# Attention products on 64 by 64 quarters of the matmul array, two groups of rows a step

## The chip, the cores and the metric

The kernel runs on one core of a Trainium2 chip. The metric is the device time of one launch in microseconds (us), as the median of several runs. Five engines of the core work side by side, each with a queue of its own that it works off in order: TensorE (PE, and PEld for its weight loads), VectorE (DVE), ScalarE (ACT), GpSimd (POOL) and SyncE (SP), which issues most of the DMA transfers.

## The reference

Attention with heads mixed before and after the softmax, then two feed-forward layers.

```python
batch, n_heads, seq, head_dim = (2, 12, 448, 64)
scores = scale * np.matmul(q, k.transpose(0, 1, 3, 2))
scores = np.einsum('bhij,hg->bgij', scores, w_pre)
scores = scores - np.max(scores, axis=-1, keepdims=True)
attn = np.exp(scores)
attn = attn / (np.sum(attn, axis=-1, keepdims=True) + 1e-09)
attn = np.einsum('bhij,hg->bgij', attn, w_post)
return np.matmul(attn, v).astype(np.float32)
...
h = x @ w_in            # 896 x 768, 768 x 2048
g = h * relu6 / 6.0     # relu6 = clip(h + 3, 0, 6); the second layer: max(h, 0) + alpha * min(h, 0)
return (g @ w_out).astype(np.float32)
```

## The kernel before

The 448 query rows of each of the two batches are cut into four tiles of 120, 120, 120 and 88 rows, eight tiles `ti` in all. Attention works on **groups** of 10 query rows (`G`): 10 rows by 12 heads are 120 partitions (`GP`), and there are 90 groups (`NG`), 12 in a tile of 120 rows and 9 in one of 88.

- **Scores.** `qk` (L193) makes the scores of one head for one tile, 448 keys wide. The products are in float32r, in two matmuls that add into one bank: keys and queries are split beforehand into a rounded part and a rest (`split_k` L150, `split_k0` L156, `split_q` L165, on DVE and POOL), stacked on 128 partitions. The first tile, and half of the second, use `qk0` (L187): one plain float32 matmul over 64 partitions, the even heads on partitions 0 to 63 and the odd ones on 64 to 127. ACT copies each head out of the bank into the tile `S` (L599, L532).
- **Pull.** `pull` (L209) moves one group from `S` (query row on the partition) to 120 partitions of row and head, by a DMA from on-chip memory to on-chip memory that SP issues.
- **Mix.** `premix` (L225) multiplies a group by the 120 by 120 matrix `wpre`, which holds `w_pre` ten times on its diagonal, into a bank `mx` (two of them); DVE takes the negated maximum (L227); `exp` (L235) is one ACT instruction and a read of its running sum.
- **Post-mix.** `norm` (L216 to L219, DVE) scales the block-diagonal `wpost` by the reciprocal sums, and `post` (L245) multiplies: the weights are 112 keys of `e`, the moving operand the 120 columns of `wr`, four matmuls a group, into a bank `pt` (two); ACT copies it to `MT` (L258), now with keys on the partitions.
- **Values.** `av` (L282) multiplies `MT` by `v` for a pair of heads `a`: four blocks of 112 keys, the two heads in the two column halves of the array. Every three pairs are copied to `xT` (L295, DVE; for the last two tiles L290 and L291).

float32 matmuls are recorded as two instructions each ("passes" below). The main loop `for s_ in range(-PL, NG + LAG)` runs one step for each group, in code order on every engine: `premix(s_)`, the scores of about one head for the next tile, `exp(s_)`, the copies, `norm(s_ - 1)`, `post(s_ - 3)`. All six `av` of a tile stand in one step, five steps after the tile's last group. In the last steps of the loop, matmuls of the first feed-forward layer (`mm3`, L446) are put in; then come the two layers, float32r in three matmuls, which the diff leaves as they are.

Of the kernel before, what the change touches and what calls it, by code (L numbers as in the profile page):

```python
# [7 lines left out]
F32 = mybir.dt.float32  # L8
# [9 lines left out]
LAG = 3  # L18
PL = 4
# [16 lines left out]
def kernel(  # L36
# [15 lines left out]
    nc = tc.nc  # L52
# [24 lines left out]
    NTILE, NG = len(tiles), len(groups)  # L77
    tps = NTILE // B
# [22 lines left out]
    with tc.manual_schedule():  # L101
        xT = xtp.tile([128, KD, NT], F32, name="xT")
        k_st, v_t, q_st = {}, {}, {}

        def load_k(b, c):
            t = kq.tile([128, HC, S], F32, tag="kst", bufs=2, name="kst")
            nc.sync.dma_start(out=t, in_=k[b - 1, :, HC * c:HC * (c + 1), :])
            k_st[b, c] = t


        def load_k0(p, z, q=nc.sync):
            c = p // HC
            if (0, c) not in k_st:
                k_st[0, c] = kq.tile([128, HC, S], F32, tag="kst", bufs=2, name="kst")
            q.dma_start(out=k_st[0, c][:, p - HC * c:z - HC * c, :], in_=k0[:, p:z, :])

        load_k0(0, 1, nc.scalar)
# [4 lines left out]
        def load_q0(c):  # L122
            n = tiles[0]["n"]
            t = q_st[0, c] = kq.tile([128, HC * GP], F32, tag="qst", bufs=3, name="qst")
            for o in range(2):
                src = q[0, D * o:D * o + D, 2 * HC * c * n:2 * HC * (c + 1) * n]
                nc.sync.dma_start(  # L127
                    out=t[D * o:D * o + D, :HC * n].rearrange("p (j x) -> p j x", j=HC),
                    in_=src.rearrange("p (j o x) -> p j o x", j=HC, o=2)[:, :, o, :],
                )  # L130

        def load_v(b, c):
            t = late.tile([JP, HC, NJ, D], F32, tag=f"v{c}", bufs=1, name=f"v{c}")
            nc.sync.dma_start(out=t, in_=v[b, :, HC * c:HC * (c + 1)])
            v_t[b, c] = t

        def load_q(ti, c):
            T = tiles[ti]
            n = HC * T["n"]
            t = kq.tile([128, HC * GP], F32, tag="qst", bufs=3, name="qst")  # L140
            a = T["i0"] * H + c * n
            nc.sync.dma_start(out=t[:, :n], in_=q[T["b"], :, a:a + n])
            q_st[ti, c] = t

        kT = [None] * H
        qT, S_t, MT = {}, {}, {}

        def split_k(b, h):  # L150
            src = k_st[b, h // HC][:, h % HC, :]
            t = kT[h] = kq.tile([128, S], R, tag=f"kT{h}", name=f"kT{h}")
            nc.vector.tensor_copy(t, src)
            nc.gpsimd.tensor_tensor(t[D:], src[D:], t[D:].bitcast(F32), ALU.subtract)

        def split_k0(h):  # L156
            a, z = (0, D) if h % 2 == 0 else (D, 2 * D)
            src = k_st[0, h // 2 // HC][a:z, h // 2 % HC, :]
            t = kT[h] = kq.tile([128, S], R, tag=f"kT{h}", name=f"kT{h}")
            nc.gpsimd.tensor_scalar(t[a:z], src, 1.0, 1.0, ALU.mult, ALU.mult)  # L160
            nc.vector.tensor_tensor(
                t[D - a:2 * D - a], src, t[a:z].bitcast(F32), ALU.subtract
            )

        def split_q(ti, c, eng=nc.gpsimd):  # L165
            n = HC * tiles[ti]["n"]
            s = q_st.pop((ti, c))[:, :n]
            t = kq.tile([128, 2, HC * GP], R, tag="qT", bufs=3, name="qT")
            eng.tensor_scalar(t[:, 0, :n], s, 1.0, 1.0, ALU.mult, ALU.mult)
            eng.tensor_tensor(t[:, 1, :n], s, t[:, 0, :n].bitcast(F32), ALU.subtract)  # L170
            qT[ti, c] = t

        def qk_out(ti, h, other):
            n = tiles[ti]["n"]
            if h == 0:
                S_t[ti] = (s_odd if ti % 2 else s_even).tile([128, H, S], F32, tag="S", name="S")
            p = (psA if other else psB).tile(
                [GP, 512], F32, tag="mx" if other else "sc", bufs=2, name="sc"
            )
            return n, p  # L180


        def qk0(ti, h):
            n, p = qk_out(ti, h, h % 2)
            o, j = D * (h % 2), h // 2
            c, a = (h // HC, h % HC) if ti else (j // HC, j % HC)
            nc.tensor.matmul(  # L187
                p[:n, :S], q_st[ti, c][o:o + D, a * n:(a + 1) * n],
                k_st[0, j // HC][o:o + D, j % HC, :], start=True, stop=True,
            )  # L190
            return (S_t[ti][:n, h, :], p[:n, :S])

        def qk(ti, h, other=False):  # L193
            n, p = qk_out(ti, h, other)
            t = qT[ti, h // HC]
            a = (h % HC) * n
            for o in range(2):
                nc.tensor.matmul(  # L198
                    p[:n, :S], t[:, o, a:a + n], kT[h], start=(o == 0), stop=(o == 1)
                )  # L200
            return (S_t[ti][:n, h, :], p[:n, :S])
# [575 lines left out]
```

## Time and profile before

| | us |
|---|---|
| median of 3 runs (701.15 to 703.30) | 702.01 |
| profiled execution, its own time | 700.6 |
| its span, first to last instruction | 698.7 |
| PE busy in the span | 689.4 (99%) |
| ACT busy | 372.3 (53%) |
| DVE busy | 438.6 (63%) |
| POOL busy | 322.2 (46%) |

The profiled execution's 700.6 us and its span differ by 1.9 us that lie around the instructions. Busy shares are means over stages of different kind: the attention loop runs from the first `premix` at 17.9 us to the last `av` at 244.5 us, and what follows is the two layers.

### The profile page before, as it was taken

The page shows a single profiled execution, that of the slowest core. Times are in us where ns is not written, and L with a number is a line of the kernel's source. Part 1 is how long each engine was busy: PE and PEld are TensorE (multiplying, and loading weights), DVE is VectorE, ACT ScalarE, POOL GpSimd, SP SyncE. Part 2 cuts the span into 40 slices and gives each one's busy share as a digit, 9 for nine tenths or more (in the row PEclk, how much of TensorE's full clock was granted, in tenths as well). Part 3 has the DMA queues.
Part 4 walks back from the last instruction along what each step waited for, and adds up shares of the span by engine and source line. Part 5 has one row for each costly group of instructions (what it writes and reads, how often), then busy time and mean ns, then how long its engine had stood idle before and what let it go on. Part 6 is the DMA issues. An engine that isn't in the chain of part 4 may idle for free.

```text
span 698.7 us, 11159 instructions
## 1 busy us (share of the span) xinstructions
PE 689.4 (99%) x4164; PEld 608.6 (87%) x4164; DVE 438.6 (63%) x778; ACT 372.3 (53%) x692; POOL 322.2 (46%) x222
## 2 busy tenths in 40 slices
PE   7999999999999999999999999999999999999998
PEld 3678878878778999999999999999999999999997
DVE  5565884456765558888873454359999999435311
ACT  5785575676866656566544443344544444444300
POOL 6321652212225344555567554534555455775630
PEclk9999999999999999999999999999999999999999
DMA  5486543364536113323234423222223223445302
GB/s 153 172 222 193 187 122 115 128 176 158 189 63 162 46 46 118 110 94 132 91 135 136 137 91 135 91 91 90 91 95 130 94 91 104 154 149 186 119 1 79
DMA packets 31874, 85.20 MB, mean 122 GB/s; under 512 B 5966, under 2 KB 21966, under 8 KB 31822
## 3 DMA queue, kind: packets, MB, share of 16 engines
q1 hardware_dynamic: 31678, 84.28, 37.9%
q8 instruction: 33, 0.54, 0.3%
q10 hardware_dynamic: 144, 0.23, 0.1%
q14 instruction: 19, 0.16, 0.1%
HBM read 62.47 MB, written 2.75 MB: 93 GB/s over the span
## 4 chain that ended last, share of the span: by engine, by line
PE 88%; POOL 4%; issue 3%; DMA 1%; DVE 1%; ACT 1%; SPq 1%; POOLq 0%
PE p L446 59%; PE pt L245 10%; PE mx L225 9%; PE av L282 5%; PE sc L198 4%; POOL wb L369 2%; POOL wlo L380 2%; DMA kst<-in_k_dram 1%; SPq L209 0%; DVE nm L227 0%; ACT S L532 0%; DMA qst<-in_q_dram 0%; SPq L127 0%; DVE wr L219 0%; ACT xh L441 0%
## 5 line engine op out<-in xcount | busy, mean ns | idle before, releaser
L380 POOL TENSOR_TENSOR wlo<-wb,whi 128x768 fp32r<-128x768 f32 x64 | 126.3, 1974 | 128.8 <-ACT whi L374 128.8
L369 POOL TENSOR_TENSOR wb<-wb,wst 128x768 int32<-128x768 int32 x64 | 125.5, 1962 | 98.0 <-DVE wb L362 80.9
L446 PE MATMUL p<-xh,whi 128*128 128x448 f32 x384 | 141.8, 369 | 0.0
L446 PE MATMUL p<-gl,whi 128*128 128x448 f32 x384 | 139.6, 363 | 0.0
L446 PE MATMUL p<-xl,whi 128*128 128x448 f32 x384 | 139.6, 363 | 0.0
L446 PE MATMUL p<-gh,whi 128*128 128x448 f32 x384 | 139.3, 363 | 0.0
L446 PE MATMUL p<-gh,wlo 128*128 128x448 f32 x384 | 138.5, 361 | 0.1
L446 PE MATMUL p<-xh,wlo 128*128 128x448 f32 x384 | 138.4, 360 | 0.0
L354 DVE TENSOR_SCALAR wb<-wb 128x768 f32<-128x768 f32 x64 | 52.4, 819 | 81.7 <-ACT wb L346 81.6
L346 ACT ACTIVATE wb<-wst 128x768 f32<-128x768 f32 x64 | 57.8, 902 | 69.1 <-DMA wst<-in_w_out_dram 53.0
L245 PEld LDWEIGHTS pt<-wr,e 120*112 120x112 f32 x720 | 86.9, 176 | 7.3 <-issue 2.0
L235 ACT ACTIVATE e<-mx,nm 120x448 f32<-120x448 f32 (+1 forms) x90 | 57.3, 637 | 59.4 <-DVE sm L216 46.5
L245 PE MATMUL pt<-wr,e 120*112 120x120 f32 x720 | 88.5, 266 | 0.0
L225 PE MATMUL mx<-pull,wmix_pre 120*120 120x448 f32 x180 | 83.5, 546 | 1.1 <-ACT e L235 1.1
L227 DVE TENSOR_REDUCE nm<-mx 120x1 f32<-120x448 f32 (+1 forms) x90 | 55.9, 621 | 44.1 <-PE mx L225 44.0
L374 ACT CAST whi<-wb 128x768 fp32r<-128x768 f32 x64 | 53.3, 833 | 50.5 <-PE p L446 32.3
L446 PEld LDWEIGHTS p<-xh,whi 128*128 128x128 f32 x384 | 72.1, 188 | 6.6 <-issue 1.2
L446 PEld LDWEIGHTS p<-gh,whi 128*128 128x128 f32 x384 | 72.1, 188 | 5.6
L446 PEld LDWEIGHTS p<-gh,wlo 128*128 128x128 f32 x384 | 71.9, 187 | 5.5 <-POOL wlo L380 0.5
L446 PEld LDWEIGHTS p<-xh,wlo 128*128 128x128 f32 x384 | 71.9, 187 | 5.1
L446 PEld LDWEIGHTS p<-xl,whi 128*128 128x128 f32 x384 | 72.2, 188 | 4.7 <-issue 0.7
L446 PEld LDWEIGHTS p<-gl,whi 128*128 128x128 f32 x384 | 72.1, 188 | 3.6
(52 smaller groups left out, 894.5 us busy)
## 6 DMA issues: line engine op xcount, KB each, us to landing
wst<-in_w_in_dram SPq DMA_DIRECT2D x32, 768.0 KB
wst<-in_w_out_dram SPq DMA_DIRECT2D x32, 768.0 KB
pull<-S SPq DMA_DIRECT2D x88, 210.0 KB
qst<-in_q_dram SPq DMA_DIRECT2D x20, 180.0 KB
kst<-in_k_dram SPq DMA_DIRECT2D x5, 672.0 KB
v<-in_v_dram SPq DMA_DIRECT2D x8, 336.0 KB
out_dram<-o SPq DMA_DIRECT2D x12, 224.0 KB
qst<-in_q_dram SPq DMA_DIRECT2D x8, 132.0 KB
```

What stands on the lines that cost most here:

```text
L198: nc.tensor.matmul(p[:n, :S], t[:, o, a:a + n], kT[h], start=(o == 0), stop=(o == 1))
L225: nc.tensor.matmul(m[:pn, :S], wpre[:pn, :pn], d[:pn], start=True, stop=True)
L227: nc.vector.tensor_reduce(nm[:pn], m[:pn, :S], axis=AX.X, op=ALU.max, negate=True)
L235: nc.scalar.activation(out=e[:pn], in_=m[:pn, :S], func=ACTF.Exp, bias=nm[:pn], accum_out=sm[:pn])
L245: nc.tensor.matmul(p[:, c * GP:(c + 1) * GP], e[:pn, c * JP:(c + 1) * JP], wr[:pn], start=True, stop=True,)
L282: nc.tensor.matmul(p[64 * o:64 * o + 64, a % 3, :n], v_t[T["b"], h // HC][:, h % HC, c, :], MT[ti][:, c, h, :n], start=(c == 0), stop=(c = ...
L346: nc.scalar.activation(t, s[:, :, 1].bitcast(F32), ACTF.Abs)
L354: nc.vector.tensor_scalar(t, t, W_MAX, W_MIN, ALU.min, ALU.max)
L369: nc.gpsimd.tensor_tensor(n, n, st_t.pop(i)[:, :, 0].bitcast(I32), ALU.add)
L374: nc.scalar.copy(hi, b_t[i])
L380: nc.gpsimd.tensor_tensor(lo, b_t.pop(i), w_t[i][0].bitcast(F32), ALU.subtract)
L446: nc.tensor.matmul(p, wt[a], xt[c], start=(first and z == 0), stop=(last and z == 2))
```

## The change

All four products of attention become plain float32 matmuls on quarters of the array, 64 by 64: the row half is set by the partitions that the operands lie on, the column half by the partitions of the bank that is written. One step now handles a pair of groups (45 steps, `NP`), and the lag from a pair's `exp` to its `post` is one step.

- `qk` handles two heads: the even one on partitions 0 to 63, the odd one on 64 to 127, each in two matmuls of up to 64 query rows for the two column halves, each head into a bank of its own. The splitting of queries and keys goes, and with it their doubled loads; both batches' keys stay in memory. `s_out` copies the even head on ACT and the odd head on DVE.
- `pull` writes a group as two halves of 5 rows by 12 heads (60 partitions), in two DMAs; the two groups of a pair lie on the two partition halves. `wpre` is 60 by 60, on both halves.
- `premix` makes four matmuls a pair, one in each quarter; each group has a bank.
- `norm` scales a 60-column `wpost` for each group. `post` makes 32 matmuls a pair, 60 columns wide, with 64 or 56 keys as weights, spread over all quarters; the five rows of each half go to a bank of their own, and two ACT copies take them to `MT`.
- `av` splits the 112 keys of a block into 56 and 56, on the two partition halves, each summed in a bank of its own: 16 matmuls a pair of heads instead of 8. ACT copies the one bank to `xT`, and DVE adds the other. The six `av` of a tile are spread over the steps, about one in each.

```diff
-LAG = 3
-PL = 4
+Q = 64
...
+    JH = JP // 2
...
+    G2 = G // 2
+    GH = G2 * H
+    WP = GH
...
+    NP = NG // 2
...
+        def qk(ti, j, tag="sc"):
+            n, m = tiles[ti]["n"], half(ti)
...
+            pool_ = psB if tag == "sc" else psA
+            ps = [pool_.tile([128, 512], F32, tag=tag, bufs=2, name="sc") for _ in range(2)]
+            t = q_st[ti, j // HC]
+            for a, z, r in ((0, Q, 0), (m, n, Q)):
+                for o in range(2):
+                    nc.tensor.matmul(
+                        ps[o][r:r + z - a, :S], t[D * o:D * o + D, j % HC, a:z],
+                        k_st[tiles[ti]["b"]][D * o:D * o + D, j, :], start=True, stop=True,
+                    )
+            w = Q + n - m
+            return [(S_t[ti][:w, 2 * j + o, :], ps[o][:w, :S]) for o in range(2)]
...
+            if g % 2 == 0:
+                d_t[g // 2] = late.tile([128, 2, S], F32, tag="pull", bufs=4, name="pull")
+            r = Q * (g % 2)
+            for c in range(2):
+                x = min(G2, xn - c * G2)
+                a = Q * c + o if st > 1 else Q + o - half(ti) + c * G2
+                src = S_t[ti][bass.ds(a, x, step=st)] if st > 1 else S_t[ti][a:a + x]
+                nc.sync.dma_start(d_t[g // 2][r:r + x * H, c, :], src)
...
+        def premix(p):
+            d = d_t.pop(p)
+            ms = []
+            for o in range(2):
+                ms.append(psA.tile([128, 512], F32, tag="mx", bufs=2, name="mx"))
+            for c in range(2):
+                for o in range(2):
+                    x = min(G2, groups[2 * p + o][3] - c * G2) * H
+                    a = Q * o
+                    nc.tensor.matmul(
+                        ms[o][Q * c:Q * c + Q, :S], wpre[a:a + x], d[a:a + x, c, :],
+                        start=True, stop=True,
+                    )
+            nms = []
+            for m in ms:
+                nm = late.tile([128, 1], F32, tag="nm", bufs=4, name="nm")
+                nc.vector.tensor_reduce(nm, m[:, :S], axis=AX.X, op=ALU.max, negate=True)
+                nms.append(nm)
+            mx_t[p] = ms, nms
...
+            for o in range(2):
+                e = late.tile([128, S], F32, tag="e", bufs=4, name="e")
+                nc.scalar.activation(
+                    out=e, in_=ms[o][:, :S], func=ACTF.Exp, bias=nms[o], accum_out=sm[:, o:o + 1]
+                )
+                e_t[2 * p + o] = e
...
+                wr = wr_t[2 * p + o] = late.tile([128, WP], F32, tag="wr", bufs=4, name="wr")
+                nc.vector.tensor_scalar(wr, wpost, sm[:, o:o + 1], None, ALU.mult)
...
+        def post(p):
+            ts = pt_t[p] = [psA.tile([128, 512], F32, tag="pt", bufs=2, name="pt") for _ in range(2)]
+            for o in range(2):
+                e, wr = e_t.pop(2 * p + o), wr_t.pop(2 * p + o)
+                for t in range(NJ):
+                    for z in range(2):
+                        for c in range(2):
+                            a, j = Q * c, t * JP + z * JH
+                            m = min(Q, S - j)
+                            u = (o * NJ + t) * GH
+                            nc.tensor.matmul(
+                                ts[c][Q * z:Q * z + m, u:u + GH], e[a:a + GH, j:j + m], wr[a:a + GH],
+                                start=True, stop=True,
+                            )
...
+            for c in range(2):
+                s = ts[c][:Q + JH, :2 * NJ * GH].rearrange("p (o u x) -> p u o x", o=2, x=G2)
+                if two[0][0] == two[1][0] and two[1][2] > 1:
+                    ti, o, _, _ = two[0]
+                    d = MT[ti][:Q + JH, :, :, o * G:(o + 2) * G].rearrange("p t g (o x) -> p (t g) o x", o=2)
+                    nc.scalar.copy(d[..., c * G2:(c + 1) * G2], s)
+                    continue
...
+                av_ps[0] = [psA.tile([128, 3, GP], F32, tag="av", bufs=2, name="av") for _ in range(2)]
...
+            for t in range(NJ):
                 for o in range(2):
-                    h = 2 * a + o
-                    nc.tensor.matmul(
-                        p[64 * o:64 * o + 64, a % 3, :n], v_t[T["b"], h // HC][:, h % HC, c, :],
-                        MT[ti][:, c, h, :n], start=(c == 0), stop=(c == NJ - 1),
-                    )
+                    for z in range(2):
+                        h = 2 * a + o
+                        nc.tensor.matmul(
+                            p[z][64 * o:64 * o + 64, a % 3, :n],
+                            v_t[T["b"], h // HC][Q * z:Q * z + JH, h % HC, t, :],
+                            MT[ti][Q * z:Q * z + JH, t, h, :n], start=(t == 0), stop=(t == NJ - 1),
+                            skip_group_check=True,
+                        )
             if a % 3 == 2:
+                c0 = T["b"] * S + T["i0"]
+                x = xT[:, a - 2:a + 1, c0:c0 + n]
+                for (d, s0), (_, s1) in zip(by_row(x, p[0][:, :, :n], n), by_row(x, p[1][:, :, :n], n)):
+                    nc.scalar.copy(d, s0)
+                    nc.vector.tensor_tensor(d, s1, d, ALU.add)
...
+                at_ = {-2: [0, 1], -1: [2], 0: [3], 1: [4], 3: [5]}
+            else:
+                at_ = spread(list(range(H // 2)), lo, hi)
...
+        def s_out(pairs):
+            for o, (d, s_) in enumerate(pairs):
+                (nc.vector.tensor_copy if o else nc.scalar.copy)(d, s_)
...
+            if 0 <= p_ < NP:
+                premix(p_)
+            pend = [qk(ti, j, "mx" if p_ < 0 and j == 1 else "sc") for ti, j in qk_at.get(p_, [])]
+            if 0 <= p_ < NP:
+                exp(p_)
+            for two in pend:
+                s_out(two)
+            if 0 <= p_ < NP - 2:
+                pull(2 * p_ + 5)
+            if 0 <= p_ < NP:
+                norm(p_)
+            if 1 <= p_:
+                post(p_ - 1)
+                post_evac(p_ - 1)
...
+            for ti, a in av_at.get(p_, []):
+                av(ti, a)
```

On PE, before, in the middle of the second tile: two steps and the start of a block of values. `sc` are scores, `mx` the mix, `pt` the post-mix, `av` the value products; a row is one or several matmuls, with the result's shape.

```order
L225 MATMUL mx<-pull,wmix_pre 120x448
L198 MATMUL sc<-kT_165,qT 120x448 x2
L245 MATMUL pt<-wr,e 112x120 x4
L225 MATMUL mx<-pull,wmix_pre 120x448
L198 MATMUL sc<-kT_171,qT 120x448 x2
L245 MATMUL pt<-wr,e 112x120 x4
L282 MATMUL av<-MT,v_419 64x120 x9
```

After the change, one step there with one pair of heads of `av`, and the mix of the next step:

```order
L190 MATMUL mx<-pull,wpre 64x448 x4
L161 MATMUL sc<-kst,qst 64x448 x2
L161 MATMUL sc<-kst,qst 60x448 x2
L229 MATMUL pt<-wr,e 64x60 x14
L229 MATMUL pt<-wr,e 56x60 x2
L229 MATMUL pt<-wr,e 64x60 x14
L229 MATMUL pt<-wr,e 56x60 x2
L275 MATMUL av<-MT,v_449 64x120 x16
L190 MATMUL mx<-pull,wpre 64x448 x4
```

A step of the new order holds two groups' mix, two heads' scores, two groups' post-mix (of the pair before), and at most places one pair of heads of values, which no longer stand six in a row.

On DVE, after the change, around the place where three pairs of heads of values are taken out (`xT`): the end of one step and the next.

```order
L197 TENSOR_REDUCE nm<-mx 128x1 x2
L532 COPY S<-sc 124x448
L213 TENSOR_SCALAR sm<-sm 128x2
L214 RECIPROCAL sm<-sm 128x2
L217 TENSOR_SCALAR wr<-wpost,sm 128x60 x2
L286 TENSOR_TENSOR xT<-av,xT 128x3x120
L197 TENSOR_REDUCE nm<-mx 128x1 x2
```

And on ACT at the same place:

```order
L206 ACTIVATE e,sm<-mx,nm 128x448 x2
L532 COPY S<-sc 112x448
L245 COPY MT<-pt 120x48x2x5 x2
L285 COPY xT<-av 128x3x120
L206 ACTIVATE e,sm<-mx,nm 128x448 x2
```

The addition `xT<-av,xT` stands on DVE ahead of the next pair's maxima, and needs ACT's copy `xT<-av`, which stands behind the copies of `pt`; before, DVE alone took the values out.

## Rows read from the trace of the kernel before

**Rows 1.** The page: span, busy time of PE and the granted clock in 40 slices.
```profile
span 698.7 us, 11159 instructions
PE 689.4 (99%) x4164; PEld 608.6 (87%) x4164; DVE 438.6 (63%) x778; ACT 372.3 (53%) x692; POOL 322.2 (46%) x222
PEclk9999999999999999999999999999999999999999
```
**Rows 2.** Attention loop: length, busy time (and instructions) by engine, clock, DMA share, GB/s.
```profile
core 0: us, PE busy (x) PEld busy (x) DVE busy (x) ACT busy (x) POOL busy (x), PEclk, DMA share, GB/s
17.90:244.50 226.60, 225.10 (x1879) 180.91 (x1878) 138.54 (x406) 156.07 (x380) 72.86 (x83) 1.00 0.51 149
```
**Rows 3.** The chain that ended last, from 60 us: start, us, engine and line.
```profile
61.45 0.75 PE mx L225 x2
62.20 0.41 PE sc L198 x2
62.61 0.82 PE pt L245 x8
63.43 0.75 PE mx L225 x2
```
**Rows 4.** Groups by line and shape: count, busy us, mean ns of one, idle before.
```profile
L225 PE MATMUL mx<-pull,wmix_pre 120*120 120x448 f32 x176 | 81.6, 547 | 1.1 <-ACT e L235 1.1
L245 PEld LDWEIGHTS pt<-wr,e 120*112 120x112 f32 x704 | 85.0, 176 | 7.2 <-issue 2.0 <-ACT MT L258 0.8
L282 PEld LDWEIGHTS av<-MT,v 112*64 112x64 f32 x768 | 36.8, 137 | 1.1 <-issue 0.3
L282 PE MATMUL av<-MT,v 112*64 112x120 f32 x576 | 30.9, 267 | 0.0
```
**Rows 5.** PE in order of time: a block of values; its start, 51.2 to 52.2 us.
```profile
52.16 5.14 PE L282 MATMUL av<-MT,v 112*64 112x120 f32 x96
...
52.16 0.14 PEld L282 LDWEIGHTS av<-MT,v 112*64 112x64 f32 x2
52.16 0.33 PE L282 MATMUL av<-MT,v 112*64 112x120 f32 x2
```
**Rows 6.** PE in order of time, 9.9 to 13.2 us: first-tile scores over 64 rows.
```profile
10.18 3.18 PE L187 MATMUL sc<-kst,qst 64*120 64x448 f32 x12 [0.24 <-DMA kst<-in_k_dram]
```
**Rows 7.** ACT and DVE in order of time, one step.
```profile
51.76 0.63 ACT L235 ACTIVATE e<-mx,nm 120x448 f32<-120x448 f32 x1 [0.36 <-DVE sm L216]
52.29 0.19 ACT L235 ACTIVATION_READ_ACCUMULATOR e<-mx,nm 120x1 f32 x1
52.38 0.52 ACT L599 COPY S<-sc 120x448 f32<-120x448 f32 x1
52.80 0.58 ACT L258 COPY MT<-pt 112x480 f32<-112x480 f32 x1
...
51.04 0.62 DVE L227 TENSOR_REDUCE nm<-mx 120x1 f32<-120x448 f32 x1 [0.78 <-PE mx L225]
```
**Rows 8.** First steps of the loop: mix, maximum, exponential, next mix.
```profile
18.96 1.38 DVE L227 TENSOR_REDUCE nm<-mx 120x1 f32<-120x448 f32 x2 [1.63 <-PE mx L225]
19.62 0.63 ACT L235 ACTIVATE e<-mx,nm 120x448 f32<-120x448 f32 x1 [1.07 <-DVE nm L227]
20.16 0.19 ACT L235 ACTIVATION_READ_ACCUMULATOR e<-mx,nm 120x1 f32 x1
20.40 1.01 PE L225 MATMUL mx<-pull,wmix_pre 120*120 120x448 f32 x2 [0.72 <-ACT e L235]
```
**Rows 9.** The last two tiles' values, taken out by ACT and DVE; groups by shape.
```profile
L291 DVE TENSOR_TENSOR xl<-av,xh 128x360 fp32r<-128x360 f32 x2 | 1.0, 526 | 6.5 <-ACT xh L290 6.5
L290 ACT CAST xh<-av 128x360 fp32r<-128x360 f32 x2 | 0.8, 463 | 5.1 <-DMA pull<-S 5.1
```
**Rows 10.** SP's pulls: duration ns min/median/max of an issue.
```profile
L209 SPq DMA_DIRECT2D pull<-S x90: 715/794/2657, 14.1 to 217.6; - x90
```

More of the change, by code (lines that the diff above doesn't have):

```diff
@@ L102, with load_k @@
         xT = xtp.tile([128, KD, NT], F32, name="xT")
[L103 to L108, printed above, removed]
-        def load_k0(p, z, q=nc.sync):
[L112 to L115, printed above, removed]
+        v_t, q_st = {}, {}
+        k_st = [kq.tile([128, H // 2, S], F32, tag=f"k{b}", name="kst") for b in range(B)]
+        def load_k0(p, z, q=nc.sync):
+            q.dma_start(out=k_st[0][:, p:z, :], in_=k0[:, p:z, :])
+        def load_k(b, o, p, z):
+            src = k[b - 1, D * o:D * o + D].rearrange("p (j o) s -> p j o s", o=2)
+            nc.sync.dma_start(out=k_st[b][D * o:D * o + D, p:z, :], in_=src[:, p:z, o, :])
+        wraw = late.tile([128, WP], F32, tag="wraw", bufs=1, name="wraw")
+        nc.gpsimd.memset(wraw, 0.0)
+        wpre = late.tile([128, Q], F32, tag="wpre", bufs=1, name="wpre")
+        nc.gpsimd.memset(wpre, 0.0)
+        wpost = late.tile([128, WP], F32, tag="wpost", bufs=1, name="wpost")
         load_k0(0, 1, nc.scalar)
@@ L183, in qk0 @@
[L183 to L186, printed above, removed]
-            nc.tensor.matmul(
[L188 to L201, printed above, removed]
+            t = late.tile([128, HC, NJ, D], F32, tag=f"v{c}", bufs=1, name=f"v{c}")
@@ L216, in norm, with exp @@
+        def exp(p):
+            ms, nms = mx_t.pop(p)
+            sm = sm_t[p] = late.tile([128, 2], F32, tag="sm", bufs=2, name="sm")
+            for o in range(2):
[4 more added lines that the diff above has]
+                e_t[2 * p + o] = e
+        def norm(p):
+            sm = sm_t.pop(p)
             nc.vector.tensor_scalar(sm, sm, 1e-9, None, ALU.add)
@@ L230, in exp @@
-        def exp(g):
-            pn = groups[g][3] * H
-            m, nm = mx_t.pop(g)
-            e = late.tile([GP, S], F32, tag="e", bufs=LAG + 1, name="e")
-            sm = late.tile([GP, 1], F32, tag="sm", name="sm")
-            nc.scalar.activation(
-                out=e[:pn], in_=m[:pn, :S], func=ACTF.Exp, bias=nm[:pn], accum_out=sm[:pn]
-            )
-            e_t[g], sm_t[g] = e, sm
-        def post(g):
-            pn = groups[g][3] * H
-            e, wr = e_t.pop(g), wr_t.pop(g)
-            p = psA.tile([JP, 512], F32, tag="pt", bufs=2, name="pt")
-            for c in range(NJ):
-                nc.tensor.matmul(
-                    p[:, c * GP:(c + 1) * GP], e[:pn, c * JP:(c + 1) * JP], wr[:pn],
-                    start=True, stop=True,
-                )
-            pt_t[g] = p
@@ new lines, in post_evac @@
+        def post_evac(p):
+            ts = pt_t.pop(p)
+            two = [groups[2 * p + o] for o in range(2)]
+            for ti, *_ in two:
+                if ti not in MT:
+                    MT[ti] = late.tile([128, NJ, H, GP], F32, tag="MT", bufs=2, name="MT")
+            for c in range(2):
[5 more added lines that the diff above has]
+                    continue
+                for k_, (ti, o, st, xn) in enumerate(two):
+                    x = min(G2, xn - c * G2)
+                    r = (o * G if st > 1 else o) + c * G2
+                    d = MT[ti][:Q + JH].rearrange("p t g x -> p (t g) x")
+                    nc.scalar.copy(d[:, :, r:r + x], s[:, :, k_, :x])
@@ L314 @@
+            hi = tiles[ti + 2]["s"] // 2 + 1 if ti + 2 < NTILE else lo + 3
+            for p_, js in spread(list(range(H // 2)), lo, min(hi, lo + H // 2)).items():
+                av_at.setdefault(p_, []).extend((ti, a) for a in js)
         P = {}
@@ L565 @@
         at(NG + 1, lambda: conv_round(3))
-        last = NG - PL - 1
+        last = NG - 6
         n1 = tiles[-2]["i0"]
```

232 lines of the change are left out of this document (70 added, 162 removed).

## The prediction

> **What bounds the kernel now.** I read the page first: PE is busy in 99% of the span, and the granted clock is full in every slice [rows 1]. So the question for any change is which part of PE's stream gets shorter, and who is late once it does. The loop of attention takes 226.6 us, and PE is busy in 225.1 of them, ACT in 156, DVE in 139 [rows 2]. The chain that ended last shows what a step of PE consists of [rows 3]: 0.75 us for the mix (two passes of 448 columns, 0.376 each), 0.41 for one head's scores (two float32r matmuls), 0.82 for the post-mix (eight passes of 120 columns, 0.102 each). Nothing stands between them; a step takes 1.98 us, and 90 of them with eight blocks of values at 5.1 us [rows 5] are nearly the whole loop. The last block lies at its end. The rest of the span, the two layers, isn't touched: I leave it as it is.
>
> How do matmuls share the array already? Two rows answer. A block of values is 96 passes of 120 columns in 5.14 us [rows 5]. Their two heads write different column halves, and two passes start together: 0.051 us a pass, half of the post-mix's 0.102 for as many columns. So two column halves run side by side at full rate. The scores of the first tile lie on 64 partitions, even heads on one row half and odd ones on the other: 12 passes of 448 columns take 3.18 us, the last one's drain included [rows 6], where one after the other would need 12 times 0.376, 4.5 us. So two row halves run side by side too. What no row shows is all four quarters at once, and nothing here asks PE for more than one weight load and one matmul in 0.051 us.
>
> **The change, part by part.** With four quarters side by side, a part costs its passes times its pass time, over four.
>
> Mix: before 90 groups at 0.75, 67.5 us. After, a pair needs 4 matmuls, 8 passes of 0.376, two deep in each quarter: 0.75 a pair, 33.8 us. **Minus 33.8.**
>
> Scores: six heads of the second tile are made before the loop's first mix, before and after. 78 heads at 0.405 [rows 3] are 31.6 us. After, 39 pairs of heads, each 8 float32 passes, two deep: 0.75, 29.3. **Minus 2.3.** The splits on POOL and DVE fall away; neither was waited for by PE in the middle of the loop, so I count nothing.
>
> Post-mix: before 90 at 0.82, 73.8. After, 32 matmuls a pair, 64 passes of 60 columns. Sixteen lie behind each other in a quarter; a pass streams 0.050 us (half of 0.102), and its weights have 64 columns. A load of 112 columns takes 176 ns and one of 64 takes 137 [rows 4], 0.8 ns a column, so 64 columns occupy 0.052 us. Lower bound: 16 times 0.053, 0.85 a pair. Upper bound: the densest stretch seen, 0.051 a pass for all 64 [rows 5], 3.3. These ends are far apart. In the block of values two loads are over in 0.14 us, where one takes 0.137, and two matmuls in 0.33, where one takes 0.27 [rows 4, 5]: they start almost at once, and it is the array that makes the pace. So I stay near the lower end: 1.0 a pair, 45 us. **Minus 28.8**, bounds minus 35.5 and plus 75.
>
> Values: 16 passes for a pair of heads in two column halves become 32 in four quarters: 0.82 before and after. **Zero**; bound plus 39 (48 pairs of heads, at 0.051 a pass 1.64).
>
> Sum on PE: minus 64.9 us.
>
> What comes back: PE is no longer alone. A pair's way through the engines is: mix until the maximum can start 1.0, maximum 0.62 [rows 7], exponential 0.05 later, 0.62 until the second may follow [rows 7], 0.73 for that with its sum's read, and 0.05 until the next mix, which needs both banks [rows 8]: 3.1 us. A full step of PE (0.75 + 0.75 + 1.0 + 0.82) is 3.3, so PE leads there. By the tables that spread them, eleven steps have no values to compute (2.5) and seven no scores (2.6): 11 times 0.6 and 7 times 0.5, **10 us back**. ACT needs two exponentials (1.25), a score copy (0.42), two copies of post-mix (about 0.49 each with the overlap of neighbours) and shares of value copies: 2.8 a step, not the bound.
>
> At 14 places of the loop the values are taken out by an ACT copy (0.46) and then a DVE addition (0.53) [rows 9], both new in their form. On DVE the addition is ahead of the next pair's maxima. On ACT the copy comes behind the exponentials (over at 3.0), the score copy and the two post-mix copies, so it ends at 4.9, and the addition at 5.4. The next maxima could have begun at 3.3 + 1.0 = 4.3. They run 1.1 late; the pair's next mix would come at 5.4 + 2.07 = 7.5 instead of 6.6: 0.8 lost, **12 us back** over 14 places. One step holds two score products for one pair of banks, which must wait for the copies behind the exponentials: 2 us. The five pairs with a tile's edge need four shorter post-mix copies, the last pair has little beside it: 2 more. **4 us back.**
>
> SP issues two pulls for each group instead of one, 0.72 to 0.79 us apiece so far for 120 rows [rows 10]. At 60 rows I take half; at the full price four of them, 2.9, and the query loads still fit within about 3.3. They are issued two pairs ahead, some 6 us. Zero; bound plus 6.
>
> 700.6 − 64.9 + 26 = 661.7 us, against the profiled execution's own time, which lies 0.2% under the median of 702.0: I say 662.
>
> **The rule that speaks against it.** The Trainium skill, TensorEngine Tiling (Array Packing), Performance Considerations, Instruction Overhead, gives each matmul about 60 cycles and warns: "Don't take tiling factor from a dimension that's already small". The post-mix here falls from 120 to 60 columns. If that charge were paid one after the other, an estimate from the page is 25 ns a matmul instruction, 64 of them 1.6 us a pair. The trace neither confirms nor refutes it: two passes start almost at once [rows 5], but no row shows more than two.
>
> **Rivals.**
> *A, a price per pass across all quarters, but small.* At half of the densest pace seen, 0.0256 a pass, the post-mix takes 1.64 a pair, 73.7, its gain gone; values stay at 0.82. PE's step is 4.0, longer than every chain above, so only the 4 us come back: 700.6 − 33.8 − 2.3 − 0.1 + 4 = 668. For it: 64 passes of 60 columns is denser than anything here. This is what the page's rule would do too.
>
> *B, slower: the same price, large.* Loop and tail have 2880 post-mix and 1536 value passes. At a price c each they cost 4416c, before they cost 73.8 + 39.4 = 113.2. The other terms gain 36.1 and give back 4. It decides from c = 145 / 4416 = 0.033 us on: below, the kernel is faster. At c = 0.051, the densest proven, 226.5 + 36: 700.6 + 113.3 − 32 = 782. Against it: in the values' block the pace is that of 120 columns streaming, not of the queue.
>
> *C, slower: two quarters at a time, not four*, because column halves exclude row halves. Mix no gain, scores 39 times 1.50 (plus 27), post-mix 32 times 0.053, 1.7 a pair (plus 2.5), values plus 39, and 4: 773. For it, only that no row shows four; against it, each kind of half runs at full rate by itself.
>
> *D, more comes back.* Maxima, additions and norms on DVE, and banks in pairs with nothing spare, make each step hand over to the next one; if all 45 steps, not 14, lost the 0.8, 25 more would come back: 687.
>
> *E, no change*: the gains of mix and post-mix eaten to the last by such waits.
>
> **How the numbers follow.** Forecast 0.43, its own range 648 to 667 (post-mix between 0.85 and 1.2 a pair, the give-back between 15 and 30); A 0.20, 663 to 672; D 0.14, 670 to 700; B 0.12; C 0.08; E 0.03. Under 0.3% a measurement here can't tell from no change. Faster: 0.43 + 0.20 + 0.14 = 0.77; same 0.03; slower 0.20. Range: from 643, all gains at their bounds with half of the give-back, up to 705, which leaves out most of B and C.
>
> **What would show it.** In the changed profile: a mix of four matmuls and the scores take 0.75 us on PE each, their eight passes in two ranks of four. The post-mix's 64 passes span about 1.0 us; at 1.6 A is right, at 3 B. If passes of different column halves on different row halves start one behind the other, C. PE's idle time should stand before the mix, with ACT's exponential as releaser, and DVE's maxima in one step of three should be released late, by the addition. I am wrong if the post-mix's passes are spaced by more than 0.033 us, or if PE idles for more than some 30 us of the loop.

## The result: 1.4% slower, where 5.7% faster was forecast

| | median, us | range |
|---|---|---|
| before | 701.66 | 701.15 to 703.30 |
| after | 711.45 | 710.89 to 712.43 |
| ratio | 1.0137 | interval 1.0116 to 1.0158 |

The profiled execution of the changed kernel took 710.89 us, with a span of 709.1. Its page, for the lines of [rows 1] and the chain that ended last:

```profile
span 709.1 us, 17560 instructions
PE 671.9 (95%) x7464; PEld 567.8 (80%) x7464; DVE 426.3 (60%) x714; ACT 359.4 (51%) x672; POOL 261.8 (37%) x148
PEclk9999999999997899999999999999999999999999
PE 70%; DMA 10%; SPq 7%; issue 4%; POOL 4%; ACT 3%; DVE 1%; POOLq 0%; DVEq 0%; ACTq 0%
```

PE does less, 671.9 us for 689.4, but it stands idle for 37.2 us of the span where it stood for 9.3. The chain now holds 10% of transfers and 7% of SP's issuing. Where nothing is late, the chain shows the step that the prediction worked out (start, us, engine and line; a pair, so twice the step of [rows 3]):

```profile
99.50 0.75 PE mx L190 x8
100.25 0.75 PE sc L161 x8
101.00 0.93 PE pt L229 x64
101.93 0.83 PE av L275 x32
```

That is 3.26 us, 3.3 by the forecast. Earlier in the loop the same chain looks like this:

```profile
60.12 0.72 SPq L179
60.85 0.04 issue
60.89 0.65 SPq L115
61.55 0.04 issue
61.59 8.20 DMA pull<-S
69.79 0.02 issue
69.81 6.95 DMA pull<-S
76.75 0.04 issue
76.80 0.59 PE mx L190
```

PE's mix comes at the end of two waits for pulls, each 7 or 8 us long from issue to landing; a pull was counted on to land within the 6 us of its lead. SP's issues of the pulls answer to [rows 10]:

```profile
L179 SPq DMA_DIRECT2D pull<-S x180: 720/742/2342, 14.1 to 221.1; - x180
```

Half the rows cost SP 742 ns, where the whole cost 794. And their time on the DMA engines is no shorter either. The stretch from 17 to 18 us holds pulls and hardly anything else; the last two columns are the mean busy share of the 16 DMA engines and GB/s. Before, then after:

```profile
17.00:18.00 1.00, 1.00 (x4) 0.34 (x3) 0.33 (x1) 0.55 (x2) 0.00 (x0) 1.00 0.65 249
```
```profile
17.00:18.00 1.00, 0.91 (x2) 0.19 (x2) 0.00 (x0) 0.00 (x0) 0.00 (x0) 1.00 0.33 125
```

A pull of 120 rows is 215 KB and takes 0.86 us at 249 GB/s, with some ten engines busy (0.65 of 16). A pull of 60 rows is 107.5 KB and takes the same 0.86 us at 125 GB/s, with five. In the trace's packet records a row of 1792 bytes takes an engine 74 ns, and in 16 to 18 us mostly ten rows are in flight at once before, and five after; the records don't name the engine. So each engine moves twelve rows, one after another (12 x 74 ns = 0.89 us). A pull reads 10 query rows before and 5 after: in these two kernels the number of engines is that of the query rows. The Trainium skill, DMA: Bandwidth & Descriptors, has the rule (under "Why a DMA increments its semaphore by 16 and not by 1"): the number of engines is the largest, up to 16, that divides the slowest dimension of both sides. It gives 10 for 10 and 120, and 5 for 5 and 60; these traces agree, with 0.65 and 0.33 of 16. The prediction did not look there.

### The profile page after: what moved, and what is told of

Same layout as the page of the kernel before. It is cut to its first block, busy times and chain, and to the rows that moved or that the text cites. A ratio compares the mean times of both kernels' runs of the same rounds, so it can differ in the third digit from the quotient of the medians.

```text
span 709.1 us, 17560 instructions
## 1 busy us (share of the span) xinstructions
PE 671.9 (95%) x7464; PEld 567.8 (80%) x7464; DVE 426.3 (60%) x714; ACT 359.4 (51%) x672; POOL 261.8 (37%) x148
## 4 chain that ended last, share of the span: by engine, by line
PE 70%; DMA 10%; SPq 7%; issue 4%; POOL 4%; ACT 3%; DVE 1%; POOLq 0%; DVEq 0%; ACTq 0%
PE p L441 58%; DMA pull<-S 10%; PE mx L190 4%; SPq L179 4%; PE pt L229 3%; PE av L275 3%; POOL wb L364 2%; PE sc L161 2%; POOL wlo L375 2%; SPq L134 2%; ACT e L206 1%; ACT MT L245 1%; SPq L142 1%; DVE nm L197 1%; DMA wraw<-in_w_post_dram 0%
## 5 line engine op out<-in xcount | busy, mean ns | idle before, releaser
L190 PE MATMUL mx<-pull,wpre 60*64 60x448 f32 x360 | 92.2, 570 | 20.3 <-DMA pull<-S 15.5
L206 ACT ACTIVATE e<-mx,nm 128x448 f32<-128x448 f32 x90 | 56.5, 631 | 67.5 <-DVE nm L197 67.3
L197 DVE TENSOR_REDUCE nm<-mx 128x1 f32<-128x448 f32 x90 | 53.5, 620 | 50.7 <-PE mx L190 46.3
L229 PEld LDWEIGHTS pt<-wr,e 60*64 60x64 f32 (+1 forms) x2880 | 67.4, 137 | 16.0 <-issue 9.8
L161 PE MATMUL sc<-kst,qst 64*64 64x448 f32 (+2 forms) x384 | 69.0, 579 | 7.4 <-DMA qst<-in_q_dram 3.9
```

What stands on the lines that cost most here:

```text
L161: nc.tensor.matmul(ps[o][r:r + z - a, :S], t[D * o:D * o + D, j % HC, a:z], k_st[tiles[ti]["b"]][D * o:D * o + D, j, :], start=True, stop= ...
L190: nc.tensor.matmul(ms[o][Q * c:Q * c + Q, :S], wpre[a:a + x], d[a:a + x, c, :], start=True, stop=True,)
L197: nc.vector.tensor_reduce(nm, m[:, :S], axis=AX.X, op=ALU.max, negate=True)
L206: nc.scalar.activation(out=e, in_=ms[o][:, :S], func=ACTF.Exp, bias=nms[o], accum_out=sm[:, o:o + 1])
L229: nc.tensor.matmul(ts[c][Q * z:Q * z + m, u:u + GH], e[a:a + GH, j:j + m], wr[a:a + GH], start=True, stop=True,)
```

## The experiments

Three theories at first. **S**: SP's issuing of four pulls a pair binds. **L**: a pull lands too late for a lead of two pairs. **H**: the hand-over between PE, DVE and ACT binds, and pulls only look late. After the packet records, **Q**: the pulls' time in the queue, 0.86 us each on five engines. The ratios below are to the kernel before.

### Other queues, and an earlier issue

```diff
-                nc.sync.dma_start(d_t[g // 2][r:r + x * H, c, :], src)
+                (nc.gpsimd if c else nc.sync).dma_start(d_t[g // 2][r:r + x * H, c, :], src)
```

> The second pull of each group (the half for the column half 1) is issued by GpSimd instead of SyncE; nothing else differs. Theory S (SyncE's issuing is the bound: 180 pulls at 0.785 us from start to start and 173 us of issues in 205 us of loop, so pulls can't get ahead of PE): SyncE's share of a step falls from 3.1 us of pulls to 1.6, PE leads again at 3.3 a step, 665 to 680 us. Rival L (the landing of a pull, 4 to 5 us after its issue, against a lead of two pairs): landing does not get shorter, 700 to 711. Rival H (the hand-over between DVE, ACT and the mix's banks): no change, 711.

Measured 710.7 us (710.4 to 711.4), ratio 1.0126 (1.0111 to 1.0141): no gain. But POOL's pulls are carried differently: in the packet records as packets of 5376 bytes that take 0.33 to 0.35 us each in the mean, and they land 5.6 us after their issue in the median. With ACT in POOL's place (`nc.scalar if c`):

> The second pull of each group is issued by ScalarE instead of SyncE. Theory S: SyncE is relieved as with GpSimd, but ScalarE pays two issues a step; if they hold its instructions up for 0.74 us each its step grows from 2.8 to 4.3, 690 to 705 us; if they run beside them, 665 to 680. Rival L: 700 to 711. Rival H: slower than 711, since ScalarE is in the chain.

Measured 728.1 (727.0 to 729.1), ratio 1.0377 (1.0359 to 1.0396). PE's waits for pulls do fall, to 5.0 us from the changed kernel's 15.5, but ACT pays for its part itself, and PE's waits for ACT's exponentials and post-mix copies come to 28 us, from 2. So neither run isolates SP's issuing. ACT's issues:

```profile
L179 ACTq DMA_DIRECT2D pull<-S x90: 749/752/1647, 14.5 to 238.6; - x90
```

A third kernel issues each pull as soon as its tile's scores and a free buffer allow (a table `pull_at` in place of the fixed two pairs):

> All pulls stay on SyncE, two a group, but each is issued as soon as the scores of its tile are copied and its buffer is free, up to two groups earlier than in the changed kernel. Theory S: SyncE issues as many, so little changes, 700 to 711 us. Rival L: the lead grows from two pairs to three, and a landing of 4 to 5 us is hidden, 670 to 690. Rival H: 711.

Measured 717.4 (713.8 to 718.0), ratio 1.0210 (1.0181 to 1.0238): 6 us slower than the changed kernel. The longer lead made nothing better; that L falls is shown by the next run, where it allowed 700 to 708.

### Fewer and shorter pulls

```diff
-            for c in range(2):
+            for c in range(1):
...
-                        ms[o][Q * c:Q * c + Q, :S], wpre[a:a + x], d[a:a + x, c, :],
+                        ms[o][Q * c:Q * c + Q, :S], wpre[a:a + x], d[a:a + x, 0, :],
```

> The changed kernel with the pulls of the second half of each group left out (90 pulls of 60 rows instead of 180); the mix reads the first half's rows for both quarters, so part of the scores is not used, and PE does every pass that it did. Theory S+Q (what binds is the pulls' time on SP and in its queue, two of about 0.8 us for each group): the steps fall to PE's own 3.3 us, and with the late start (4.7 us) and the sums at the end (some 5 us) the time is 662 + 10 = 672, range 655 to 685. Rival H (the hand-over on DVE and ACT and the two mix banks hold the steps, the pulls only look late): the same work is handed over, so no gain, 705 to 712. Rival L (landing time against a lead of two pairs): a pull lands about as late after its issue as before, so a small gain, 700 to 708.

Measured 677.2 us (675.0 to 679.5), ratio 0.9645 (0.9618 to 0.9671): 34 below the changed kernel with the same work on every engine but SP and the DMA engines. H as the first bound falls, and L.

Where the 34 us lie can be read at the mix, in the changed kernel and then in this run (busy us, mean ns of one, then idle time before):

```profile
L190 PE MATMUL mx<-pull,wpre 60*64 60x448 f32 x360 | 92.2, 570 | 20.3 <-DMA pull<-S 15.5
```
```profile
L190 PE MATMUL mx<-pull,wpre 60*64 60x448 f32 x360 | 61.1, 549 | 13.2 <-ACT e L206 7.6
```

The same 360 passes stand 31 us longer in the profile's busy time, and wait 7 us more. A pair's four mix matmuls come one by one as the pulls land, and PE counts as busy while one of them runs alone: in the step at 53.57 us of the changed kernel the eight passes are spread over 2.4 us, and a weight load among them waits 0.74 us for a pull. Most of the loss is thus inside PE's 671.9 us of busy time (643.2 with half the pulls, for as many passes), not in its idle time.

```diff
-                nc.sync.dma_start(d_t[g // 2][r:r + x * H, c, :], src)
+                nc.sync.dma_start(d_t[g // 2][r:r + x * H, c, :], src[..., :S // 2])
```

> The changed kernel with all 180 pulls, each of 60 rows, but of the first 224 keys alone (896 bytes a row instead of 1792); the mix reads these columns twice, so half of the scores is not used, and PE does every pass that it did. It tells two parts of the pulls' cost apart. Theory S (SP's 0.74 us of issuing for each of four pulls in a pair, whatever it moves): no gain, 705 to 712. Theory Q (a 60-row pull's rows are moved by five DMA engines, 12 rows one after another on each at 74 ns, 0.85 us in the queue, where 120 rows took ten engines and the same 0.85 us): the rows take less than 74 ns each, about 40 to 50, so the queue needs some 0.5 us a pull, and SP's 0.78 from issue to issue is what is left: 4 x 0.78 = 3.1 and the loads, a small gain at most to 690 to 703. Rival H: 705 to 712.

Measured 691.65 (690.3 to 694.5), ratio 0.9856 (0.9829 to 0.9882). The issues are the same in number and price (737 ns); the time on the engines alone changed (41 ns a row instead of 74 in the packet records, 0.47 us a pull), and 20 us came back. So the greater part of the 34 is the engines' time, and about 14 hangs on the issues that remain, or on half of the bytes that do.

The same on the kernel before: each pull cut into two of 60 rows (`for c in range(2)` over halves of the group's rows), or into two of 120 rows by half of the keys.

> The kernel before, with each group's pull cut into two DMAs of 60 rows (48 in the last group), as the changed kernel issues them; nothing else of the change. Theory S: SyncE's issues in the loop rise from 100 to some 167 us of 205; the old kernel issues four groups ahead and its step is 1.98, two pulls 1.57 plus loads 0.3, so it just fits: 702 to 712 us. If the second issue came for half of a whole one, as the prediction took it: 702. Rivals L and H: 702.

Measured 721.7 (720.6 to 727.7), ratio 1.0299 (1.0255 to 1.0343): 20 us, with no edit on PE.

> The kernel before with each pull cut into two of 120 rows by 224 keys, so that the issues double as in the run with two pulls of 60 rows (721.7), while ten DMA engines still share each. Theory S (issuing binds): as that run, 718 to 725. Theory Q (the time in the queue binds): two pulls of 12 rows x 40 to 50 ns take about 1.0 to 1.2 us of queue for a group, against 0.85 in the kernel before and 1.7 in the two-pull run, which fits in its step of 1.98: 701 to 706.

Measured 709.2 (708.4 to 709.9), ratio 1.0103 (1.0086 to 1.0121): between the two. By these two runs, doubled issues cost some 7 us there (or the queue time, which by 24 rows of 41 ns is 0.98 us a group instead of 0.86), and five engines in place of ten another 12 or 13; Q alone, which allowed 706 for the second run, is not the whole. PE's waits for the pulls in the two runs, in us, times and the longest, the one with five engines first:

```profile
PE mx L227 <- DMA pull<-S: 9.3, 8, 1.9
```
```profile
PE mx L227 <- DMA pull<-S: 1.3, 4, 0.6
```

### What else is on those engines

By itself a pair's four pulls need 3.4 us against PE's 3.26, which is nearly enough room. Four stretches of the loop, as in [rows 2], show where it wasn't; the changed kernel, then the run with half the pulls:

```profile
17.90:60.00 42.10, 37.25 (x739) 19.30 (x739) 23.40 (x64) 24.28 (x61) 0.00 (x0) 1.00 0.47 153
60.00:100.00 40.00, 33.86 (x888) 21.96 (x887) 21.25 (x59) 24.06 (x60) 0.00 (x0) 1.00 0.47 140
100.00:140.00 40.00, 39.45 (x1194) 30.21 (x1190) 26.69 (x76) 29.20 (x77) 0.00 (x0) 1.00 0.36 115
140.00:180.00 40.00, 33.44 (x890) 21.36 (x882) 23.00 (x61) 25.47 (x64) 1.85 (x1) 1.00 0.53 170
```
```profile
17.90:60.00 42.10, 39.09 (x1039) 26.80 (x1042) 28.59 (x82) 30.96 (x80) 0.00 (x0) 1.00 0.51 149
60.00:100.00 40.00, 37.45 (x1163) 29.55 (x1159) 25.50 (x73) 28.00 (x72) 0.00 (x0) 0.96 0.24 70
100.00:140.00 40.00, 36.12 (x1151) 27.44 (x1146) 27.48 (x79) 31.02 (x84) 0.00 (x0) 1.00 0.44 130
140.00:180.00 40.00, 34.25 (x1019) 25.02 (x1015) 26.93 (x72) 28.73 (x71) 6.39 (x4) 1.00 0.29 93
```

From 100 to 140 us the changed kernel gets through as many passes as the other, 1194 and 1151. It falls behind until 100 us (1627 passes against 2202), while values and keys are being loaded besides the queries, and again after 140, when the second batch's values and the layers' first weights come. Those loads stand between the pulls in SP's queue:

```profile
44.51 3.15 SPq L179 DMA_DIRECT2D pull<-S  x4
47.71 0.93 SPq L142 DMA_DIRECT2D v<-in_v_dram  x2
48.68 3.14 SPq L179 DMA_DIRECT2D pull<-S  x4
```

From 39.5 to 64.7 us SP issues without a gap, one pair's pulls every 4.3 us, where PE needs 3.26. Does the loads' place in the queue matter? The loop's loads went to POOL, in the changed kernel, in the run with two kinds of pairs and in the wide mix (both told below):

```diff
-            nc.sync.dma_start(out=k_st[b][D * o:D * o + D, p:z, :], in_=src[:, p:z, o, :])
+            loader[0].dma_start(out=k_st[b][D * o:D * o + D, p:z, :], in_=src[:, p:z, o, :])
...
+        loader[0] = nc.gpsimd
         for p_ in range(-2, NP + 1):
```

> The changed kernel with the loop's loads of queries, keys and values issued by POOL, which has no other work in most of the loop; SP's queue then holds pulls alone. Theory S+Q with the loads as a part of it (four pulls of 0.85 us and a load or two between them, together above PE's 3.26 us): the pulls alone need 3.4 us a pair, just above PE, so most of the loss is gone, 685 to 700 (677 is what half the pulls gave). If the pulls by themselves are the bound, loads or not: 705 to 712. Rival: loads on another queue share the five engines with the pulls, which then take longer than 0.85 us each: 708 to 716.

Measured 707.9 (705.2 to 709.9), ratio 1.0087 (1.0055 to 1.0120): 3.5 us below the changed kernel.

> The run with two kinds of pairs (703.3), with the loop's loads on POOL. There the pulls need 2.6 us a pair on average and PE 3.9, and yet its longest waits are pulls that land 8 us after their issue, behind key and value loads in the same queue (65 us into the run). If the loads are what stood ahead of them: 680 to 695. If not: 700 to 706.

Measured 706.9 (706.0 to 710.3), ratio 1.0086 (1.0054 to 1.0117): no gain over 703.3.

> The wide-mix kernel (695.8) with the loop's loads on POOL. Its steps run at PE's 4.52 us with no wait for a pull beyond 1.2 us in all, so no change, 693 to 698; if POOL's issuing delays the values' or queries' arrival, up to 5 us slower.

Measured 707.0 (704.5 to 709.8), ratio 1.0082 (1.0053 to 1.0111): the control lost 11 us. POOL ran ahead, and the first pulls of the changed kernel met its loads. Chain, then the DMA share of that stretch:

```profile
19.29 16.00 DMA pull<-S
```
```profile
20.00:25.00 5.00, 3.14 (x6) 0.60 (x6) 0.00 (x0) 0.00 (x0) 2.31 (x4) 0.50 0.84 199
```

From 20 to 40 us the changed kernel with its loads on POOL gets through 76 passes (330 with them on SP), but from 40 to 80, with most loads behind it, through 1018 (830). So POOL was held to the steps, by a copy of one column of the last maxima ahead of each step's loads (`nc.gpsimd.tensor_copy(pace, last_nm[0])`).

> The changed kernel with the loop's loads on POOL (707.9), and POOL now copies one column of the last pair's maxima ahead of each step's loads, so that a load is not issued before the step that issued it so far. In the run without, POOL waited for nothing, issued the first batch's values, two tiles' queries and keys between 11 and 25 us, and the first pulls stood behind them (16 us for one). Theory S+Q with the loads as a part: the late start goes, some 11 us as the control lost there, 692 to 700. If the loads' place in the queue is not a part of it: 705 to 711.

Measured 718.2 (715.6 to 720.7), ratio 1.0239 (1.0203 to 1.0275): slower than with all on SP.

> The run with two kinds of pairs and the loads on POOL (706.9), paced in the same way. With the loads as a part of the pulls' wait: 690 to 698, the best run if PE's mean of 3.9 to 4.0 a pair comes through. If not: 701 to 707.

Measured 707.4 (704.7 to 710.8), ratio 1.0091 (1.0056 to 1.0127): no gain either.

> The wide mix with the loads on POOL (707.0), paced in the same way: control. Its 11 us over the wide mix with the loads on SP (695.8) should go, if they came from the early loads: 693 to 698.

Measured 700.4 (697.4 to 704.3 in nine runs, a tenth took 708.5), ratio 0.9993 (0.9971 to 1.0015): above 693 to 698, so the early loads were not all of the 11 us. In no kernel did loads that run at the same time as the pulls cost less in POOL's queue than in SP's, so their place in SP's queue is not shown to be the cost; what they cost on the engines was not isolated. In the changed kernel with the paced loads a pull's row takes 91 ns in the mean from 33 to 65 us in the packet records, where it takes 78 in the changed kernel from 30 to 58, and the chain of the first half is one pull after another:

```profile
33.60 9.92 DMA pull<-S
...
43.54 10.52 DMA pull<-S
```

### Mixing the wide way

```diff
-            for c in range(2):
-                x = min(G2, xn - c * G2)
...
-                nc.sync.dma_start(d_t[g // 2][r:r + x * H, c, :], src)
+            src = S_t[ti][bass.ds(o, xn, step=st)] if st > 1 else S_t[ti][o:o + xn]
+            nc.sync.dma_start(d_t[g // 2][:xn * H, g % 2, :], src)
...
+                nc.tensor.matmul(ms[o][:, :S], wpre[:x], d[:x, o, :], start=True, stop=True)
```

> The changed kernel with the mix of the kernel before: one pull of 120 rows for each group (90 in all), one mix matmul over the whole array for each group, its weights spread so that the results lie in the two quarters as now; a head's scores are one matmul on half of the array's rows with all their columns. Post-mix, values, exponentials and their sums stay as changed. PE's step is then 1.5 mix + 0.75 scores + 0.93 post-mix + 0.83 values = 4.0 us a pair, against 3.26 where the changed kernel's steps run undisturbed and 4.78 in the kernel before. Theories S and Q (pulls are the bound): two pulls a pair take 1.6 to 1.7 us, so the step is PE's: 45 x 4.0 = 180 instead of 215, with the late start and end 702 - 34 + 10 = 678, range 670 to 690. Rival H (hand-over binds at about 4.3 to 4.8 us a pair): 700 or more. Rival L: two pulls land sooner, so also faster, 675 to 695.

Measured 695.8 (693.3 to 696.2), ratio 0.9902 (0.9880 to 0.9923): **faster than both kernels**, and 18 us above the expectation. Its chain shows why; PE waits for pulls for 1.2 us in all, but the step's parts are longer than counted:

```profile
89.04 1.70 PE mx L182 x4
90.74 0.95 PE sc L160 x4
91.69 1.07 PE pt L218 x60
92.76 0.83 PE av L264 x32
```

4.55 us where 4.0 was expected: the mix 0.20 over two of [rows 3], scores 0.20 and post-mix 0.14 over the changed kernel's. All three follow a change between the whole array, its halves and its quarters; the values, which follow the post-mix on the same quarters, keep their 0.83. That the change itself is what costs is argued from this, not tested. The Trainium skill, TensorEngine Tiling (Array Packing), Key Properties, says that a change of the tiling mode drains the engine; 0.14 to 0.20 us a change is what these rows show. 45 pairs at 0.55 are 25 us, which more than covers the 18.

Can the two mixes be combined, so that the pulls have room? Quarters in even pairs, wide in odd ones:

> The wide-mix kernel with the changed kernel's mix (four pulls of 60 rows, four quarters) in every even pair, and the wide mix (two pulls of 120 rows) in every odd one. The pulls then need 3.4 and 1.7 us of the queue in turn, 2.6 on average and some 0.5 for loads; PE needs 3.26 and 4.55, 3.9 on average. Theories S+Q: the pulls stay below PE in the mean and are issued two pairs ahead, so PE sets the steps: at best 45 x 0.65 = 29 below the wide mix's 695.8, 667; with the hand-over's chain, which held the steps of the run with half the pulls at some 3.8 us, about 20 below, 676. Range 667 to 690. Rival L (the lead does not average the two kinds): the quarter pairs wait as in the changed kernel, 690 to 702.

Measured 703.25 (701.8 to 705.2), ratio 1.0021 (0.9996 to 1.0046). The longest piece of its chain from 60 to 75 us is again a pull, in the stretch with the loads (8.11 us from 65.18), and every pair changes the array's shape. How the 7 us over the wide mix divide between the two stays open.

> As the run with two kinds of pairs, and the sum of the two value banks (ACT's copy, DVE's addition) is taken out behind the next pair's exponentials instead of ahead of its maxima, where a block of three value pairs ends with a step. Theory H as the second bound (ACT's copies, then DVE's addition, then the maxima, then the exponentials: 0.35 + 0.53 us longer in a step with a take-out, some 14 of them): 5 to 12 us below the run without. If these take-outs never ended a wait: no difference.

Measured 709.7 (706.5 to 712.0), ratio 1.0108 (1.0075 to 1.0140): 6 us slower, where the theory had 5 to 12 faster.

> As the run with two kinds of pairs and later sums, with a wide pair only in every third place. PE then needs 3.7 us a pair in the mean (3.9 with every second one wide), the pulls 2.8 and the loads 0.5. If PE or the hand-over still bind: up to 9 us below the run with every second pair wide. If two quarter pairs in a row, 6.8 us of pulls, outrun the lead: the same or up to 8 us above it.

Measured 712.4 (709.3 to 713.2), ratio 1.0142 (1.0114 to 1.0169). With more quarter pairs, and so more pulls, it is no faster; the ranges of this run and the one at 709.7 overlap.

> As the run with half the pulls left out (677.2; the mix reads the first half's rows for both quarters, part of the scores is not used), with the value sums taken out behind the next pair's exponentials. It shows the second bound without the first. Theory H: its steps of 4.3 to 4.7 us beside those of 3.26 are the ones with a take-out, so 6 to 12 us below, 665 to 671. Otherwise 675 to 679.

Measured 683.9 (683.1 to 690.9), ratio 0.9766 (0.9720 to 0.9812): 7 us worse than without, not 6 to 12 better. The wait moved, and now the next block of values waits for its banks; that the value sums are what makes the long steps is not shown by this.

```profile
PE av L277 <- ACT xT L288: 10.0, 9, 3.1
```

## Why the prediction was wrong

**The work on PE was right.** Mix and scores take 0.75 each, the post-mix 0.93 (1.0 forecast, bounds 0.85 and 3.3), the values 0.83 (0.82). Rivals A, B and C fall with it: 64 passes in 0.93 us are 0.0145 us a pass, under the 0.033 from which B decides, and four quarters run at once. The charge for each matmul that the Trainium skill gives (TensorEngine Tiling (Array Packing), Instruction Overhead) would have made 1.6 us a pair, by the prediction's estimate, if it were paid one after the other; the row shows 0.93. One range does not follow from its own ends: post-mix 0.85 to 1.2 and give-back 15 to 30 make 644 to 675, not 648 to 667. Nothing else hangs on it.

**The step that failed** is SP's pulls: "At 60 rows I take half; at the full price four of them, 2.9, and the query loads still fit within about 3.3. They are issued two pairs ahead, some 6 us. Zero; bound plus 6." The issue did not halve (742 ns for 794), but 2.9 allowed for that. Two things were left out. The loads of values and keys stand in SP's queue too, not only those of queries, and where they come SP needs 4.3 us a pair, not 3.3. And the term counted SP's time only: a pull's 0.86 us on the DMA engines was not in it, and that did not halve either, so four need 3.4 us a pair, with the loads on top. Measured: the run with half the pulls gives 34 us back, 20 of them come back with the same issues and shorter rows, and the doubled pulls alone cost the old kernel 20. How much of the other 14 is issuing stays open. A term of nothing, with a bound of 6, came to 34, so the range's upper end, 705, was too low as well.

**The give-back of 26 was too small.** With half the pulls left out, 677 stands 15 above the forecast. There the chain is D's, maxima, exponentials and value sums one after another 4.37 us from one pair's maxima (61.29) to the next one's (65.66):

```profile
61.29 0.62 DVE nm L197
...
61.99 1.34 ACT e L206 x4
63.33 0.42 ACT S L532
63.75 1.00 ACT MT L245 x2
64.75 0.35 ACT xT L285
...
65.12 0.53 DVE xT L286
65.66 0.54 DVE nm L197
```

The addition does stand ahead of the next maxima, as the prediction said. But how the 15 divide between these steps, the ones with less to compute and a lower clock (0.96 from 60 to 100 us in that run) was not settled; the run meant to take the additions out moved the wait instead.

So 662 + 34 + 15 = 711; the two are differences of measured and forecast times, not sums of waits. The sign was lost to the first of them: at 677 the change would have been a gain. "PE idles for more than some 30 us of the loop" was named as what would show the prediction wrong. It did not show:

```profile
17.90:254.70 236.80, 209.16 (x5141) 141.95 (x5140) 129.78 (x346) 146.26 (x367) 23.74 (x19) 0.96 0.40 126
```

PE is idle for 27.6 us of the loop, since a mix that gets its pulls one by one counts as busy. The sign also looked for ACT's exponential as what releases the mix; of the 20.3 us of idle time before the mix, 15.5 end with a transfer.

## What to carry to other kernels

When a transfer is cut in two, each half may take as long as the whole did, as here: look at how many DMA engines the whole keeps busy, and add its time on them, not only its issue, to what the engines carry at that place of the program. Count every transfer that its queue issues there, and read a stretched group of matmuls as a wait, even where the profile calls it busy. A hand-over that costs nothing at one step's length can be the bound at two thirds of it, so cost every transfer again at the new step. And take the part of a change that makes the gain without the part that feeds the bound: post-mix and values on quarters with the old pulls gained 1.0%, where the whole change lost 1.4%.

## What the runs showed beside

The granted clock fell in the changed kernel's loop, where the prediction counted a full one. The end of the loop, in stretches of 10 us (PE busy first, then the granted clock ahead of the DMA share):

```profile
200.00:210.00 10.00, 9.00 (x213) 4.88 (x212) 5.33 (x17) 8.04 (x20) 4.00 (x3) 1.00 0.31 69
210.00:220.00 10.00, 6.99 (x136) 4.32 (x136) 3.59 (x9) 5.74 (x16) 6.94 (x6) 0.73 0.28 92
220.00:230.00 10.00, 9.81 (x191) 7.84 (x184) 2.30 (x9) 3.92 (x12) 1.83 (x2) 0.76 0.62 179
230.00:240.00 10.00, 7.81 (x130) 6.63 (x134) 3.64 (x10) 5.54 (x14) 3.79 (x4) 0.66 0.05 18
```

In the 30 us from 210 on PE was idle for 5.4 us, and the clock stood at its lower level, 1.2 GHz, for more than half of the time (0.73, 0.76 and 0.66 are means of the two levels). In [rows 2] the mean is 1.00. A lower clock and idle time come together here, but not everywhere: from 90 to 100 us PE was idle for 2.9 us, and the clock stayed at 1.00. The loop's mean is 0.96, and 0.98 in the run with half the pulls; an estimate from these means and PE's busy time (209 us and 181) puts the difference at up to 5 of the 34 us. No run here separates it.
